# Attention followed by eight routed experts: the routing is issued by a running estimate of VectorE's time, and two experts' products are turned by TensorE

## The chip, the cores and the metric

The kernel is written in Bass for one core of a Trainium2 chip. The metric is device time in microseconds (us) of one execution. Kernel before: 892.86 us, the median of three runs (891.03, 892.86, 893.77). Each engine (TensorE, VectorE, ScalarE, GpSimd and SyncE; PE, DVE, ACT, POOL and SP in the profile) executes its own instructions strictly in the order in which the program lists them, and waits at an instruction until what that one needs is there. So the order of each list matters, and the change is one of order.

## The reference

Sigmoid attention of 8 batches and 12 heads makes 3584 rows of 768 numbers. The rows then go to eight experts. The routing is greedy over all (row, expert) pairs in falling order of their logit, and each expert takes exactly 448 rows:

```python
    order = np.argsort(-flat)
    for idx in order:
        tok, e = (int(idx) // E, int(idx) % E)
        if assigned[tok] >= 0 or counts[e] >= cap:
            continue
        assigned[tok] = e
        counts[e] += 1
    for e in range(E):
        mask = assigned == e
        h = np.maximum(x[mask] @ w1[e], 0.0)
        out[mask] = h @ w2[e]
```

`w1[e]` is 768x1024 and `w2[e]` 1024x768, in float32.

## The kernel before

**Attention** fills the first 280 us and is not touched. It ends with the rows in DRAM (`xs`) and the logits in SBUF.

**Routing** runs in eight phases, one an expert, and each phase finds the next expert that fills up, and its 448 rows. A phase (`Router.phase`) is nearly all VectorE work with a few short TensorE operations: take the former expert's rows out and make new keys (`remove`, `keys`, L306 to L158); turn the keys (TensorE, L167) and copy them (L170); search the threshold in 16 steps (L178 to L217), each step counting how many keys lie over three candidates; then `r_kap` (L222), a TensorE transpose of it (L229), the pick (L232 to L250), positions (TensorE L257, L262, L263; VectorE L259 to L268), a one-hot table (`r_oh`, L284) that TensorE turns into lists (32 small matmuls L289, then L296), and the list of row numbers `r_idx` (L298). Phase k+1 can be issued only after phase k.

**Experts.** With a list there, four gathers on GpSimd's queue bring an expert's rows (L625, tiles `xr`). Each block of 128 rows is turned in two halves: three TensorE transposes into a PSUM tile (L639, `tp`, two buffers), ScalarE copies the rounded part out (`xh`, L642), and VectorE makes the remainder (`xl`, L643), which frees the PSUM buffer. So there are eight such turns of three transposes an expert. The first product then takes 144 matmuls (L725, L727, L729) and the second 144 (L765, L767, L769). Weights stream in over SP's queue; ScalarE and GpSimd split them (`wh` L603, `wl` L605), GpSimd also makes `hl` (L737).

**Products.** For experts 0 to 6 VectorE turns each of the three product tiles in 32x32 blocks straight out of PSUM (`turn_y`, L666), four DMAs store it to DRAM (`ys`, L672), four more read rows back (L677), and GpSimd scatters them to the output (L681). Only the last expert is turned by TensorE: a ScalarE copy (L793), and per block of rows two transposes (L652) and a ScalarE copy (L657).

**What sets the order.** The loop over `moe(kx)` lists the matmuls; each `yield` tells the matmul's price (`MM` = 189 ns) and moves a model clock. Two other streams are woven in by that clock. The routing generator yields how long its last piece is thought to last, and the next piece is listed when the clock is past the last one by that and `SLACK`:

```python
                if t >= t_route:
                    t_route = t + next(route, 0) + SLACK
```

A search step has `T_DVE` = 2025 ns. Chores (gathers, turns, stores, scatters) have due times and one is listed at most every `CHORE_NS` = 1000 ns. At the end of an expert `flush` lists every chore that the next expert needs, at once. Inside `xturn` the VectorE instruction L643 is listed right behind the transposes and the ScalarE copy that it waits for.

Of the kernel before, what the change touches and what calls it, by code (L numbers as in the profile page):

```python
# [118 lines left out]
class Router:  # L119
# [42 lines left out]
    def search(self, pe):  # L162
# [10 lines left out]
        for st in range(16):  # L173
# [45 lines left out]
            if not pe:  # L219
                yield T_DVE  # L220
# [31 lines left out]
    def place(self):  # L252
# [7 lines left out]
        yield T_TOT  # L260
# [10 lines left out]
    def lists(self):  # L271
# [10 lines left out]
        nc.vector.tensor_tensor(K.mv[:, :, :8], os, K.tok[:, :, None].to_broadcast([112, 32, 8]), OP.mult)  # L282
        oh = wk.tile([112, 64, 32], F16, name="r_oh", bufs=1)
        nc.vector.tensor_tensor(oh, K.io64, rr[:, None, :].to_broadcast([112, 64, 32]), OP.is_equal)  # L284
        yield T_OH
# [7 lines left out]
        yield T_BT  # L293
# [30 lines left out]
    def phase(self, k):  # L324
        if k:
            self.remove()
        if k < 7:
            self.keys()
            yield T_KEYS
            yield from self.search(k == 0)  # L330
            yield T_KAP
            self.pick()
        else:
            self.left()
        yield T_PICK
        yield from self.place()
        yield from self.lists()


def moe_attention(tc, q, k, v, w_gate, w1, w2, out):  # L340
# [7 lines left out]
    with contextlib.ExitStack() as ctx:  # L348
# [202 lines left out]
        def routing():  # L551
            for kx in range(E):
# [6 lines left out]
                yield 0  # L559
# [68 lines left out]
        def xturn(kx, j, n, hf, wide):  # L628
# [12 lines left out]
            sl = (slice(None), slice(hf * 3, hf * 3 + 3), slice(j * 128, j * 128 + n))  # L641
            nc.scalar.activation(xh[sl], pv, AF.Copy)  # L642
            nc.vector.tensor_tensor(xl[sl], pv, xh[sl].bitcast(F32), OP.subtract)  # L643

        scat, chores = [], []
        MM = 189

        def untranspose(kx, yr, i, yt, j, n, t0=0, end=False):

            p = R.bank() if end and j % 2 else ps_t.tile([128, 512], F32, name="tp")  # L650
# [10 lines left out]
        def turn_y(kx, i, py):  # L661
# [4 lines left out]
            nc.vector.transpose(z.rearrange("p b (j d) -> p d b j", d=2),  # L666
                                py[:, :, :S].rearrange("p d (b t) -> p d b t", t=32))
# [5 lines left out]
            return store  # L673
# [31 lines left out]
        def moe(kx):  # L705
# [3 lines left out]
            for i in range(4):  # L709
                ph = ps_s.tile([128, 2, 512], F32, name="sc")  # L710
                cuts = ((0, 256), (256, S)) if kx + i == 0 else ((0, S),)
                mm = 107 if len(cuts) > 1 else MM
# [29 lines left out]
            if kx == E - 1:  # L742
# [3 lines left out]
            for i in range(3):  # L746
                last = (kx, i) == (E - 1, 2)
                for lo, hi in (((0, 256), (256, S)) if last else ((0, S),)):
                    py = ps_s.tile([128, 2, 512], F32, name="sc")
                    w = hi - lo  # L750
                    for j in range(2):
# [5 lines left out]
                        for d2 in range(2):  # L757
                            dsl = slice(d2 * 128, (d2 + 1) * 128) if kx == E - 1 else slice(d2, 256, 2)
# [22 lines left out]
                    if kx < E - 1:  # L781
                        extra[0] += Y_NS
                        chores.append((clock[0] + Y_WAIT, kx + 2, turn_y(kx, i, py)))
                        if i == 2:
                            for j, n in blocks():
                                chores.append((clock[0] + 2 * Y_WAIT + 1000, kx + 2,
                                               lambda j=j, n=n: y_row(kx, yr, j, n)))
                            for j, n in blocks():
                                chores.append((clock[0] + Y_LATE + 2600 * j, kx + 2,
                                               lambda j=j, n=n: scatter(kx, yr, j, n)))  # L790
                        break
# [7 lines left out]
        clock, extra = [0.0], [0.0]  # L799
# [8 lines left out]
        for j, n in blocks():  # L808
            for hf in range(2):
                if j < 2:  # L810
                    xturn(0, j, n, hf, True)
                else:
# [4 lines left out]
        t_route, t_chore = FIRST, 1500.0  # L817
        for kx in range(E):
# [40 lines left out]
            flush(kx + 1)  # L859
        flush(E + 1)  # L860
# [27 lines left out]
```

## Time and profile before

| What | Value |
|---|---|
| Median of three runs | 892.86 us |
| The profiled execution: its time, and its span | 898.64 us, 896.7 us |
| PE busy, share of the span | 841.6 us, 94% |
| DVE busy | 557.1 us, 62% |
| ACT busy | 412.3 us, 46% |
| POOL busy | 466.8 us, 52% |
| Mean granted TensorE clock | 0.969 |

The sums below are made against the profiled execution. It is 5.8 us longer than the median of the runs, so what the sums give is a difference, and it is taken off the median. The span runs from the first to the last instruction. A matmul's end is modelled and matmuls overlap, so "PE busy" says little; the time between the starts of matmuls is what is used. "Granted clock" is the share of full speed at which TensorE was allowed to run.

### The profile page before, as it was taken

To read this page: it belongs to the slowest core of one execution; us is meant where nothing else is said; L and a number is where in the kernel's file an instruction comes from. 1 tells how busy PE (TensorE), PEld (TensorE's weight loads), DVE (VectorE), ACT (ScalarE), POOL (GpSimd) and SP (SyncE) were. 2 spreads that over 40 slices of the span, in tenths; PEclk is the share of its full clock that TensorE was granted. 3 is DMA by queue.
4 is the path that set the end of the run, shared out by engine and by line. 5 is a ranking of instruction groups with operands and counts; after the bars stand their busy time and mean duration, and the time that the engine had idled before them with its cause. 6 is when DMAs were issued, how large, how long until landed. Compare 5 with 4: busy or idle time off the path is not lost.

```text
span 896.7 us, 16051 instructions
## 1 busy us (share of the span) xinstructions
PE 841.6 (94%) x5339; PEld 641.5 (72%) x5339; DVE 557.1 (62%) x2076; ACT 412.3 (46%) x532; POOL 466.8 (52%) x446
## 2 busy tenths in 40 slices
PE   6999999999998849989998998998999999999996
PEld 3455555455454539978987987997998888999996
DVE  4566555555555978868678858948957975233110
ACT  6777777777775723413413412332242342451432
POOL 9744444444400026834862873595485685653561
PEclk9999999999999969998997998999899999999998
DMA  9867666666603863374465455554546646835631
GB/s 173 166 141 152 143 124 126 133 124 126 132 18 113 276 196 99 95 201 151 141 202 160 120 183 142 157 185 139 179 147 200 182 147 200 242 127 174 214 109 62
DMA packets 246066, 136.83 MB, mean 153 GB/s; under 512 B 183360, under 2 KB 232512, under 8 KB 245984
## 3 DMA queue, kind: packets, MB, share of 16 engines
q1 hardware_dynamic: 233248, 102.31, 43.7%
q0 software_dynamic: 10880, 33.28, 12.1%
q8 instruction: 42, 0.69, 0.3%
q10 hardware_dynamic: 1856, 0.23, 0.2%
q14 instruction: 40, 0.33, 0.1%
HBM read 104.10 MB, written 31.65 MB: 151 GB/s over the span
## 4 chain that ended last, share of the span: by engine, by line
PE 75%; DVE 12%; issue 6%; POOL 4%; DMA 2%; ACT 1%; SPq 0%; POOLq 0%; DVEq 0%; ACTq 0%
PE tp L457 13%; PE sc L433 11%; PE sc L727 8%; PE sc L725 8%; PE sc L729 8%; PE sc L767 6%; PE sc L765 6%; PE sc L769 5%; DVE r_junk L178 4%; PE tp L463 2%; PE sc L443 2%; POOL wl L605 2%; DVE xl L643 1%; PE tp L639 1%; PE tp L478 1%
## 5 line engine op out<-in xcount | busy, mean ns | idle before, releaser
L605 POOL TENSOR_TENSOR wl<-wr,wh 128x768 fp32r<-128x768 f32 (+1 forms) x96 | 204.2, 2140 | 84.4 <-ACT wh L603 83.8
L423 ACT ACTIVATE at<-sc,bias 128x896 f32<-128x896 f32 x168 | 161.3, 1005 | 66.8 <-PE sc L443 38.4
L383 POOL DMA_DIRECT2D nkq<-in_q_dram x188 | 118.2, 645 | 116.2 <-DVE kqT L408 104.6
L727 PE MATMUL sc<-xl,wh 128*128 128x448 f32 (+2 forms) x396 | 148.4, 375 | 3.1 <-DVE xl L643 3.1
L725 PE MATMUL sc<-xh,wh 128*128 128x448 f32 (+2 forms) x396 | 148.8, 376 | 0.0
L729 PE MATMUL sc<-xh,wl 128*128 128x448 f32 (+2 forms) x396 | 148.3, 374 | 0.0
L769 PE MATMUL sc<-hh,wl 128*128 128x448 f32 (+2 forms) x400 | 147.4, 369 | 0.0
L603 ACT ACTIVATE wh<-wr 128x768 fp32r<-128x768 f32 (+1 forms) x112 | 101.0, 936 | 99.7 <-PE sc L767 69.6
L765 PE MATMUL sc<-hh,wh 128*128 128x448 f32 (+2 forms) x400 | 145.8, 364 | 0.5 <-ACT yt L694 0.5
L767 PE MATMUL sc<-hl,wh 128*128 128x448 f32 (+2 forms) x400 | 146.2, 366 | 0.0
L178 DVE TENSOR_SCALAR_CACHE_REDUCE r_junk<-r_KE,r_T 128x224 bf16<-128x224 f32 x315 | 123.4, 442 | 0.1
L737 POOL TENSOR_TENSOR hl<-yt,hh 128x896 fp32r<-128x896 f32 x32 | 68.2, 2130 | 100.8 <-ACT yt L736 100.8
L457 PE MATMUL tp<-at,nv 128*64 128x448 f32 x576 | 118.8, 548 | 0.0
L733 ACT ACTIVATE hh<-sc 128x896 fp32r<-128x896 f32 x32 | 29.4, 919 | 152.7 <-PE sc L729 152.7
L417 DVE TENSOR_TENSOR kqL<-kqT,kqH 128x896 fp32r<-128x896 f32 (+1 forms) x49 | 52.5, 1073 | 58.3 <-ACT kqH L416 58.2
L727 PEld LDWEIGHTS sc<-xl,wh 128*128 128x128 f32 x396 | 77.9, 197 | 11.0 <-DVE xl L643 4.0
L625 POOL DMA_INDIRECT xr<-xs,r_idx x32 | 32.1, 1002 | 100.4 <-ACT wh L603 80.2
L725 PEld LDWEIGHTS sc<-xh,wh 128*128 128x128 f32 x396 | 77.9, 197 | 7.2
L729 PEld LDWEIGHTS sc<-xh,wl 128*128 128x128 f32 x396 | 77.8, 197 | 7.1
L767 PEld LDWEIGHTS sc<-hl,wh 128*128 128x128 f32 x400 | 77.8, 194 | 5.4 <-issue 1.5
L765 PEld LDWEIGHTS sc<-hh,wh 128*128 128x128 f32 x400 | 77.7, 194 | 4.6 <-ACT yt L694 0.6
L769 PEld LDWEIGHTS sc<-hh,wl 128*128 128x128 f32 x400 | 77.8, 194 | 3.6
(166 smaller groups left out, 1166.8 us busy)
## 6 DMA issues: line engine op xcount, KB each, us to landing
wr<-in_moe_w_dram SPq DMA_DIRECT2D x64, 384.0 KB, 4.2
wr<-in_moe_w_dram SPq DMA_DIRECT2D x48, 512.0 KB, 4.0
nkq<-in_k_dram SPq DMA_DIRECT2D x192, 56.0 KB, 2.6
xs<-xr SPq DMA_DIRECT2D x32, 336.0 KB, 3.4
nkq<-in_q_dram POOLq DMA_DIRECT2D x188, 56.0 KB, 2.7
ys<-yt SPq DMA_DIRECT2D x84, 112.0 KB, 2.9
nv<-in_v_dram SPq DMA_DIRECT2D x92, 96.0 KB, 2.6
xr<-ys SPq DMA_DIRECT2D x21, 384.0 KB, 5.3
```

Source lines behind the costliest of these rows:

```text
L178: nc.vector.tensor_scalar(junk, KE, T[:, i:i + 1].bitcast(F32), None, OP.is_ge, OP.add, accum_out=cnt[:, i:i + 1])
L383: qn.dma_start(t[o:o + 32, n], rws[x])
L423: nc.scalar.activation(a, p[:, :, :S], AF.Sigmoid, bias=bias, scale=1 / math.sqrt(D))
L457: nc.tensor.matmul(p[j * 64:j * 64 + 64, :S], nat["v", b, g][:, h0 + j, c, :], AT[b, pr, c][:, j, :], start=(c == 0), stop=(c == 2 and pr ...
L603: nc.scalar.activation(hi, raw[u], AF.Copy)
L605: eng.tensor_tensor(lo, raw[u], hi.bitcast(F32), OP.subtract)
L725: nc.tensor.matmul(ph[:, f, lo:hi], wh[:, a, fs], xh[:, dd, lo:hi], start=st, stop=False)
L727: nc.tensor.matmul(ph[:, f, lo:hi], wh[:, a, fs], xl[:, dd, lo:hi], start=False, stop=False)
L729: nc.tensor.matmul(ph[:, f, lo:hi], wl[:, a, fs], xh[:, dd, lo:hi], start=False, stop=en)
L765: nc.tensor.matmul(py[:, d2, :w], wh[:, a, dsl], h1, start=st, stop=False)
L767: nc.tensor.matmul(py[:, d2, :w], wh[:, a, dsl], h2, start=False, stop=False)
L769: nc.tensor.matmul(py[:, d2, :w], wl[:, a, dsl], h1, start=False, stop=(j == 1 and a == 3))
```

## The change

1. Pacing of the routing. `T_...`, `SLACK`, `FIRST` are gone. Every piece of routing yields two numbers: what it costs VectorE, and how long VectorE then waits for TensorE. `dve[0]` is a running model of the time at which VectorE is done with all that was listed so far. `go_on` lists the next piece when the model clock is within `LEAD` (300 ns) of that time, or, where VectorE waits for TensorE, `GAP` (250 ns) past it. A search step is now two pieces, the counting at 1150 ns and the rest at 940 ns; before it was one piece.
2. The model clock: a matmul is priced at 203 ns for 189, and transposes advance the clock too.
3. VectorE's `xl` and its product transposes are listed later than the TensorE and ScalarE work that they wait for (`after`, lags of 900 and 500 ns), so that they stand between pieces of routing, and their cost goes into the model.
4. Experts 0 and 1 (`Y_FIRST` = 2) have their products turned by TensorE, as the last expert has; experts 2 to 6 as before.
5. The four gathers of the second expert (kx 1) are listed at once, not one every 1500 ns. The chore interval depends on what the last chore put on TensorE (300, 1100 or 1500 ns, for 1000).

```diff
-T_KEYS, T_KE, T_STEP, T_DVE, T_KAP, T_PICK, T_TOT, T_OH, T_BT = 3600, 2100, 2050, 2025, 500, 2600, 600, 3800, 600
-SLACK = 150
-CHORE_NS = 1000
+PE_NS, OH_NS, GAP, LEAD = 600, 1700, 250, 300
-FIRST = 4000.0
-Y_NS, Y_WAIT, Y_LATE = 1100, 5000, 29000
+Y_FIRST, Y_WAIT, Y_LATE, X_NS = 2, 5000, 29000, 1500
...
-                yield T_STEP
+                yield 0, 0
+            else:
+                yield 1150 + 430 * (st == 0), 0
+            if pe:
...
-            if not pe:
-                yield T_DVE
+            if not pe and st < 15:
+                yield 940 + 850 * (st == 0), 0
...
+        yield 2050, 0
         oh = wk.tile([112, 64, 32], F16, name="r_oh", bufs=1)
         nc.vector.tensor_tensor(oh, K.io64, rr[:, None, :].to_broadcast([112, 64, 32]), OP.is_equal)
-        yield T_OH
+        yield 2300, OH_NS
...
-            yield T_KEYS
+            yield 4600, PE_NS
             yield from self.search(k == 0)
-            yield T_KAP
+            yield 1100, PE_NS
             self.pick()
...
-        yield T_PICK
+        yield 2550, PE_NS
...
+            clock[0] += 3 * 110
             nc.scalar.activation(xh[sl], pv, AF.Copy)
-            nc.vector.tensor_tensor(xl[sl], pv, xh[sl].bitcast(F32), OP.subtract)
+
+            def low():
+                nc.vector.tensor_tensor(xl[sl], pv, xh[sl].bitcast(F32), OP.subtract)
+            after(900, 170 + n * 3, low)
...
-        MM = 189
+        MM = 203
...
+        def after(lag, cost, f):
+            later.append((clock[0] + lag - LEAD, cost, f))
+            hand_out()
+
+        def hand_out(end=False):
+            while later and (end or later[0][0] <= clock[0]):
+                _, cost, f = later.pop(0)
+                dve[0] = max(dve[0], clock[0] + LEAD) + cost
+                f()
+
+        def by_dve(kx):
+            return Y_FIRST <= kx < E - 1
...
-            if kx == E - 1:
+            if not by_dve(kx):
                 yr = [xp.tile([128, DM], F32, name="xr", bufs=XR_BUFS) for _ in blocks()]
...
-                            dsl = slice(d2 * 128, (d2 + 1) * 128) if kx == E - 1 else slice(d2, 256, 2)
+                            dsl = slice(d2 * 128, (d2 + 1) * 128) if not by_dve(kx) else slice(d2, 256, 2)
...
+        clock[0], dve[0], seg[:] = 0.0, 2400.0, [0, 2400.0]
+        t_chore = 1500.0
+
+        def go_on():
+
+            while clock[0] >= (seg[1] + GAP if seg[0] else dve[0] - LEAD):
+                cost, wait = next(route, (0, -1))
+                if wait < 0:
+                    seg[:] = 1, 1e9
+                    return
+                dve[0] = max(dve[0], clock[0] + seg[0]) + cost
+                seg[:] = wait, dve[0]
...
-                    chores.append((t0 + 1500 * j, kx + 1, lambda j=j, n=n: gather(kx + 1, j, n)))
+                    if kx:
+                        chores.append((t0 + 1500 * j, kx + 1, lambda j=j, n=n: gather(kx + 1, j, n)))
+                    else:
+                        gather(1, j, n)
...
-                t_route += extra[0]
-                extra[0] = 0.0
-                if t >= t_route:
-                    t_route = t + next(route, 0) + SLACK
+                hand_out()
+                go_on()
...
-                        t_chore = t + CHORE_NS
+                        t_chore = t + (300, 1100, X_NS)[min(2, int(clock[0] - t) // 110 - 1 if clock[0] > t else 0)]
```

What that does to the lists, at two places.

TensorE at the border between expert 0 and expert 1. `xr` are the gathered rows, `rt` routing, `yt` expert 0's products. Before, all eight turns of expert 1's rows (24 transposes) stand in one block behind the last matmul of expert 0:

```order
L769 MATMUL sc<-hh,wl 128x448
L639 MATMUL tp<-ident,xr 128x128 x18
L639 MATMUL tp<-ident,xr 128x64 x6
L725 MATMUL sc<-xh,wh 128x448
L727 MATMUL sc<-xl,wh 128x448
```

In the changed kernel the last rows there are these, and four more turns stand ahead of them, six matmuls apart:

```order
L640 MATMUL tp<-ident,xr 128x128 x3
L792 MATMUL sc<-hh,wh 128x448
L794 MATMUL sc<-hl,wh 128x448
L796 MATMUL sc<-hh,wl 128x448
...
L640 MATMUL tp<-ident,xr 128x128 x3
L640 MATMUL tp<-ident,xr 128x64 x6
L752 MATMUL sc<-xh,wh 128x448
L754 MATMUL sc<-xl,wh 128x448
L756 MATMUL sc<-xh,wl 128x448
L658 MATMUL tp<-ident,yt 128x128 x2
```

Five of the eight turns moved ahead of the border, three are left at it, and expert 0's product transposes (`yt`) are new on TensorE.

VectorE at the same border, in the search for expert 2. `r_junk` is the counting, `r_T` the next candidates. Before:

```order
L211 TENSOR_SCALAR r_T<-c_kk,r_J 128x3
L666 STREAM_TRANSPOSE yt<-sc 128x2x448
L643 TENSOR_TENSOR xl<-tp,xh 128x3x128 x6
L643 TENSOR_TENSOR xl<-tp,xh 128x3x64 x2
L178 TENSOR_SCALAR r_junk,c_CN<-r_KE,r_T 128x224 x3
```

And in the changed kernel:

```order
L175 TENSOR_SCALAR r_junk,c_CN<-r_KE,c_c_425 128x224 x3
L647 TENSOR_TENSOR xl<-tp,xh 128x3x128
L194 STREAM_TRANSPOSE r_ct<-c_CN 128x32
...
L211 TENSOR_SCALAR r_T<-c_kk,r_J 128x3
L647 TENSOR_TENSOR xl<-tp,xh 128x3x128 x2
L175 TENSOR_SCALAR r_junk,c_CN<-r_KE,r_T 128x224 x3
L647 TENSOR_TENSOR xl<-tp,xh 128x3x128
```

The eight `xl` are spread over three pieces of the search, and the product transpose is gone from VectorE's list for experts 0 and 1.

The places of the routing's TensorE operations, counted in expert matmuls from the first one, move like this (expert 0 ends at 324, and then an expert ends every 288: 612, 900, 1188, 1476, 1764, 2052):

| Phase, for expert | Keys turned (L167): before, now | `r_kap` turned (L229) | List ready (L296) | Turns at the border itself |
|---|---|---|---|---|
| 1 | before the first in both | 243, 210 | 293, 266 | 8 of 8, 3 of 8 |
| 2 | 314, 292 | 516, 470 | 572, 529 | 7, 0 |
| 3 | 593, 553 | 795, 730 | 845, 790 | 3, 0 |
| 4 | 872, 817 | 1074, 1014 | 1124, 1074 | 2, 0 |
| 5 | 1151, 1101 | 1353, 1298 | 1403, 1358 | 0, 0 |
| 6 | 1424, 1386 | 1632, 1583 | 1682, 1643 | 0, 0 |

More of the change, by code (lines that the diff above doesn't have):

```diff
@@ L259, in place @@
         nc.vector.tensor_copy(tot, p[:64, :1].to_broadcast([64, 112]))
-        yield T_TOT
+        yield 270, PE_NS
         p = self.bank()
@@ L292, in lists @@
         nc.vector.tensor_copy(bt, p[:, :64])
-        yield T_BT
+        yield 230, PE_NS
         p = self.bank()
@@ L558, in routing @@
                 R.ei = None
-                yield 0
+                yield 160, 0
         route = routing()
@@ L641, in xturn @@
             sl = (slice(None), slice(hf * 3, hf * 3 + 3), slice(j * 128, j * 128 + n))
+            clock[0] += 3 * 110
             nc.scalar.activation(xh[sl], pv, AF.Copy)
-            nc.vector.tensor_tensor(xl[sl], pv, xh[sl].bitcast(F32), OP.subtract)
+            def low():
+                nc.vector.tensor_tensor(xl[sl], pv, xh[sl].bitcast(F32), OP.subtract)
+            after(900, 170 + n * 3, low)
         scat, chores = [], []
-        MM = 189
+        MM = 203
         def untranspose(kx, yr, i, yt, j, n, t0=0, end=False):
+            clock[0] += 220
             p = R.bank() if end and j % 2 else ps_t.tile([128, 512], F32, name="tp")
@@ L659, in untranspose, with turn_y @@
                 scatter(kx, yr, j, n)
-        def turn_y(kx, i, py):
+        def after(lag, cost, f):
[8 more added lines that the diff above has]
+            return Y_FIRST <= kx < E - 1
+        def turn_y(kx, i, py, yr):
             z = hp.tile([128, 2, S], F32, name="yt", bufs=YT_BUFS).rearrange("p n t -> p (n t)")
             z = z.rearrange("p (b c) -> p b c", c=64)
-            nc.vector.transpose(z.rearrange("p b (j d) -> p d b j", d=2),
-                                py[:, :, :S].rearrange("p d (b t) -> p d b t", t=32))
             def store():
@@ L672, in store, with turn @@
                     nc.sync.dma_start(v[i, q], z[32 * q:32 * q + 32])
-            return store
+            def turn():
+                nc.vector.transpose(z.rearrange("p b (j d) -> p d b j", d=2),
+                                    py[:, :, :S].rearrange("p d (b t) -> p d b t", t=32))
+                chores.append((clock[0] + Y_WAIT, kx + 2, store))
+                for j, n in blocks() if i == 2 else ():
+                    chores.append((clock[0] + 2 * Y_WAIT + 1000, kx + 2, lambda j=j, n=n: y_row(kx, yr, j, n)))
+                for j, n in blocks() if i == 2 else ():
+                    chores.append((clock[0] + Y_LATE + 2600 * j, kx + 2, lambda j=j, n=n: scatter(kx, yr, j, n)))
+            after(500, 1150, turn)
         def y_row(kx, yr, j, n):
@@ L711, in moe @@
                 cuts = ((0, 256), (256, S)) if kx + i == 0 else ((0, S),)
-                mm = 107 if len(cuts) > 1 else MM
+                mm = 119 if len(cuts) > 1 else MM
                 for lo, hi in cuts:
@@ L780, in moe @@
                         break
[L781 to L790, printed above, removed]
+                    if by_dve(kx):
+                        turn_y(kx, i, py, yr)
                         break
@@ L797, in moe @@
                                            untranspose(kx, yr, i, yt, j, n, lo, last)))
-        clock, extra = [0.0], [0.0]
+        clock, dve, seg, later = [0.0], [0.0], [0, 0.0], []
         while 0 not in listed:
@@ L811, in moe_attention @@
                     xturn(0, j, n, hf, True)
+                    hand_out(True)
                 else:
@@ L816, in moe_attention @@
                     next(route)
-        t_route, t_chore = FIRST, 1500.0
+        clock[0], dve[0], seg[:] = 0.0, 2400.0, [0, 2400.0]
[8 more added lines that the diff above has]
+                seg[:] = wait, dve[0]
         for kx in range(E):
@@ L835, in flush @@
                     c[2]()
+                    hand_out(True)
+                hand_out(True)
             for step, cost in enumerate(moe(kx)):
@@ L859, in moe_attention @@
             flush(kx + 1)
+        hand_out(True)
         flush(E + 1)
```

## The prediction

> **What bounds the kernel now.** I read the page's slices first, then busy time by expert, the chain of waits and the list of waits, then the timeline at the places that these name.
>
> ```profile
> PE   6999999999998849989998998998999999999996
> PEclk9999999999999969998997998999899999999998
> ```
>
> TensorE is the bound throughout: its row stands at 8 and 9. In the expert part (from slice 15) the granted clock dips again and again. One stretch for each expert, first matmul to first matmul, with the instructions on the tile `sc`:
>
> ```profile
> 332.83:406.65 73.82, 64.17 (x330) 58.09 (x330) 4.81 (x6) 8.23 (x11) 0.96 0.49 143
> 406.65:480.08 73.43, 62.96 (x288) 56.01 (x288) 3.32 (x3) 6.91 (x8) 0.94 0.51 157
> 555.00:622.65 67.65, 65.03 (x288) 56.32 (x288) 2.23 (x2) 6.91 (x8) 0.96 0.59 175
> 763.72:825.55 61.83, 60.82 (x289) 54.37 (x288) 3.35 (x3) 6.91 (x8) 1.00 0.63 192
> sum 492.72, PE 448.56 PEld 392.24 DVE 23.70 ACT 49.70; mean PE 64.08 PEld 56.03 DVE 3.39 ACT 7.10
> ```
>
> Expert 6 (763.72) has the same 288 matmuls and 24 row transposes, no routing left, clock 1.00: 61.83 us. That is the floor of an expert. Experts 0 to 5 take 68 to 75. Where the difference goes shows in the chain at the border between experts 0 and 1:
>
> ```profile
> 400.29 1.11 DVE yt L666
> 401.40 0.46 DVE xl L643
> 401.90 0.56 PE tp L639 x3
> 402.48 0.50 ACT xh L642
> 403.00 0.57 DVE xl L643
> 403.62 1.38 PE tp L639 x6
> ```
>
> TensorE turns rows, ScalarE copies, VectorE subtracts, and only then is a PSUM buffer free for the next turn: a loop of 403.62 - 401.90 = 1.72 us in which TensorE works 0.38 (priced below). VectorE was late to begin with, since a product transpose stood ahead. The waits, and what they do to the clock:
>
> ```profile
> DVE r_km L232 <- PE rt L229: 34.9, 7, 8.6
> PEld tp L639 <- DVE xl L643: 18.8, 24, 2.5
> 459.87 1.13 PE L289 MATMUL rt<-r_oh,c_mv 112*32 112x64 f16 x32 [1.34 <-DVE r_oh L284]
> 532.24 1.11 PE L289 MATMUL rt<-r_oh,c_mv 112*32 112x64 f16 x32 [1.37 <-DVE r_oh L284]
> 403.70:410.60 6.90, 6.30 (x23) 5.02 (x24) 5.13 (x24) 3.11 (x6) 2.69 (x2) 0.52 0.31 86
> 461.10:464.50 3.40, 3.40 (x18) 2.94 (x19) 2.27 (x7) 0.85 (x1) 0.64 (x1) 1.00 0.18 47
> 475.40:485.70 10.30, 8.90 (x31) 7.26 (x31) 8.21 (x36) 4.08 (x8) 3.61 (x2) 0.52 0.47 121
> 533.40:536.90 3.50, 3.50 (x12) 2.67 (x12) 2.00 (x7) 0.00 (x0) 1.47 (x2) 0.55 0.19 65
> ```
>
> After the border waits the clock is at half for 6.9 us (403.70) and 10.3 us (475.40). One wait of 1.37 us was followed by 3.5 us at half clock (533.40), one of 1.34 was not (461.10). So a wait of this size may cost its own length and 1.7 us more. And VectorE waits 34.9 us in seven phases, 5 each, for TensorE to reach the turn of `r_kap`: the routing is listed later than VectorE could do it. That slack is what the change spends.
>
> **The change part by part.** Prices first:
>
> ```profile
> 771.10:778.54 7.44, 7.44 (x37) 6.76 (x37) 1.52 (x1) 3.19 (x4) 4.64 (x2) 1.00 1.01 318
> 778.54:787.50 8.96, 8.96 (x52) 8.13 (x52) 3.28 (x5) 5.16 (x8) 3.92 (x2) 1.00 0.85 241
> 796.24:825.55 29.31, 29.31 (x145) 27.95 (x145) 2.24 (x2) 1.73 (x2) 1.00 0.57 180
> 862.14:870.24 8.10, 8.10 (x44) 7.31 (x44) 0.00 (x0) 3.05 (x6) 6.49 (x10) 1.00 0.35 147
> ```
>
> Each of the first two and the last holds 36 matmuls. Twelve row transposes add 8.96 - 7.44 = 1.52, 0.127 each. 144 matmuls take 29.31, 0.2035 each; 36 are 7.33, so the 8 product transposes of the last row add 0.77, 0.19 a pair. Over an expert a matmul is (61.83 - 24 x 0.127) / 288 = 0.204. Routing puts the 32 small matmuls on TensorE (1.13 above) and four short ones, about 0.5: 1.6 a phase.
>
> *Products of experts 0 and 1 on TensorE.* 24 pairs, 4.6 us on the bounding engine. VectorE loses six transposes of 1.11. SP loses 32 transfers, ScalarE gains six tile copies and 24 row copies on an engine that is busy a third of the time in these stretches. Of the pairs 6 fall into expert 0, 13 into expert 1, 5 into expert 2.
>
> *Turns off the border.* Three of expert 1's eight turns and none of the later ones stay there. The other turns stand 6 matmuls apart, 1.22 + 0.38 = 1.6 us, about the loop's length, so they hide. I leave one unhidden loop at the first border: 1.72 - 0.38 = 1.3, and one stretch of half clock, 1.7.
>
> *The search is listed closer.* This is the part that costs. A search step is now priced 1150 + 940 = 2090 ns. What it takes:
>
> ```profile
> 611.77 0.36 PE L167 MATMUL rt<-ident,r_KT 112*128 112x112 f32 x2
> 616.43 0.44 DVE L178 TENSOR_SCALAR_CACHE_REDUCE r_junk<-r_KE,r_T 128x224 bf16<-128x224 f32 x1
> 618.75 1.01 DVE L643 TENSOR_TENSOR xl<-tp,xh 128x384 fp32r<-128x384 f32 x2
> 654.88 0.15 DVE L222 TENSOR_SCALAR r_kap<-r_J 128x1 int32<-128x1 int32 x1
> ```
>
> One step is 618.75 - 616.43 = 2.32 us, with no gap on VectorE. From the keys' turn to the end of `r_kap` are 655.03 - 611.77 = 43.26, one product transpose in it: 42.2 without (phases 2 and 3), 44.4 with two (phases 4 to 6). On TensorE's list now stand between the same two, in phase 3, 177 matmuls, 21 row transposes and 8 pairs: 36.1 + 2.7 + 1.5 = 40.3; in phases 4 and 5, 197 and 21: 42.9; in phase 6, 197 and 24: 43.2; in phase 2, 178, 24, 6 pairs and the border's wait: 41.8. So TensorE comes to `r_kap` early and waits: 0.4, 1.9, 1.5, 1.5, 1.2 us in phases 2 to 6. Before, VectorE waited. Phase 1 runs from the start:
>
> ```profile
> 332.83:344.48 11.65, 11.29 (x78) 10.46 (x79) 1.47 (x3) 1.31 (x3) 0.87 0.59 191
> 332.83:372.50 39.67, 39.31 (x216) 36.61 (x217) 1.47 (x3) 8.23 (x11) 0.96 0.45 136
> 338.75 0.56 DVE L643 TENSOR_TENSOR xl<-sc,xh 128x384 fp32r<-128x384 f32 x1 [0.83 <-ACT xh L642]
> 375.77 0.21 DVE L217 TENSOR_SCALAR r_J<-r_acc,r_J 128x1 int32<-128x1 int32 x1
> ```
>
> TensorE has done 210 matmuls (and six transposes on `sc`) at 372.5. VectorE ended its last step at 375.98; a product transpose that follows falls away, and of its early waits for `xh`, of which the row shows one of 0.83, some 1.3 us goes as counting now stands between them. So `r_kap` at 374.8 and a wait of 2.4 us, with one stretch of half clock, 1.7. What is late next: nothing, the list is ready 58 matmuls ahead of the border, not 31. For the half clock behind the 1.9 of phase 3 I add half a stretch, 0.85; the shorter ones stay near the 1.34 that had none.
>
> [...]
>
> *Gathers.* The first turn follows the list's matmul by 25 to 28 matmuls, 5.1 us and up.
>
> ```profile
> 391.58 0.20 PE L296 MATMUL rt<-c_SEL,r_bt 128*64 128x4 f16 x2
> 392.25 0.97 POOL L625 DMA_INDIRECT xr<-xs,r_idx  x1 [3.31 <-DVE rt L306]
> xr<-xs,r_idx POOLq DMA_INDIRECT x32, 4.7
> 740.83 0.20 PE L296 MATMUL rt<-c_SEL,r_bt 128*64 128x4 f16 x2
> 743.19 5.52 DMA xr<-xs,r_idx
> ```
>
> Issue 0.67 behind L296 and 4.7 to land: 5.4. Phase 7 had 2.36 + 5.52 = 7.9, behind a scatter. So 0 to 2.8 a phase; I take 0.3, near the first, and 0.3 for a late `r_oh`. Listing expert 1's gathers in a row puts blocks 1 to 3 earlier on GpSimd than their turns need, so it costs nothing; a `wl` behind them waits at most 4 issues.
>
> The sum, us:
> - Expert 0: 11.65 + 252 x 0.2035 + 1.6 + 3.05 + 6 x 0.19 + 2.4 + 1.7 + 1.3 + 1.7 = 75.8
> - Expert 1: 61.83 + 1.6 + 2.5 + 0.4 + 0.6 = 66.9
> - Expert 2: 61.83 + 1.6 + 1.0 + 1.9 + 0.85 + 0.6 = 67.8
> - Experts 3 and 4: 61.83 + 1.6 + 1.5 + 0.6 = 65.5 each
> - Expert 5, with two phases: 61.83 + 3.2 + 1.2 + 0.6 = 66.8
> - Expert 6: 61.83
>
> Together 470.1 for 492.72: 22.6 less. Expert 7 and the end stay. Taken off the median, 892.86 - 22.6 = 870.
>
> **The rivals.**
>
> *VectorE is in time after all.* Pieces listed among the waits, and `xl` between counting and the rest, could hide what the row-by-row sum doesn't. Then the picks' waits (8.9) and their half clock (2.55) go: 859. Against it: the steps run without gaps now, there is nothing to hide in.
>
> *The gathers take the border's place.* If the landing of phase 7 is the rule, TensorE waits 2.8 at the first turn of five experts and pays 1.7 of clock each time: 22.5 for my 1.5, so 891, no change to speak of. For it: turns come closer behind the list than before. Against: only one of seven first gathers was issued that late.
>
> *The pick's wait breaks the clock* (slower). TensorE's list is strict, so all matmuls behind L229 stand still in each of six phases. If each such wait is followed by 10.3 us at half clock, as at 475.40, that is 5.1 x 6 = 30.6 for my 2.55: 898. It turns slower where the half clock costs over (22.6 + 2.55) / 6 = 4.2 us a pick. For it: my waits of 1.2 to 2.4 lie around the 1.37 that tripped. Against: the long stretches followed several waits in a row.
>
> **How the numbers follow.** The forecast 0.70, VectorE in time 0.10, gathers 0.12, broken clock 0.08. A difference under 0.3% can't be told here. Forecast and first rival are faster, half of the gathers' case is within 0.3%: faster 0.86, same 0.06, slower 0.08. The range: down to 859, the first rival; up to 886, where the picks' half clock or the gathers cost 16 more than I take.
>
> **What would show it.** Right: the first matmul of expert 1 near 408 us, of expert 7 near 803; no TensorE waits on `xl` at borders 2 to 6; new waits of L229 on `r_kap`, 1 to 2.5 us in at least four phases, and hardly any of `r_km` on L229; clock dips at picks, not at borders. Wrong: `r_km` still waiting microseconds for L229 (a step is cheaper in its new place), or the first turn of each expert waiting for `xr`, or half clock longer than 3.5 us behind each pick.

## The result

| | Median, us | Lowest to highest | Runs |
|---|---|---|---|
| Kernel before | 892.19 | 891.03 to 893.77 | 4 |
| Changed kernel | 904.33 | 899.88 to 904.79 | 4 |

The changed kernel takes 1.0124 times as long, 95% interval 1.0087 to 1.0160. Forecast were 870 us, between 859 and 886: wrong in size and in sign. The profiled execution of the changed kernel took 904.54 us (span 902.8), right at its median.

Busy time and the slices of the changed kernel's page:

```profile
PE 840.3 (93%) x5387; PEld 640.0 (71%) x5387; DVE 545.1 (60%) x2070; ACT 425.6 (47%) x562; POOL 464.8 (51%) x446
PE   6999999999998749999979999989989999999996
PEclk9999999999999969999989999989999999999999
```

The dips of the border are gone from the expert part, but PE now has 7 and 8 where it had 9, and PEclk dips once in each of three experts. By expert, first matmul to first matmul (the instructions on tile `sc`, as in the prediction):

```profile
332.54:407.24 74.70, 68.23 (x330) 57.54 (x331) 1.43 (x3) 10.91 (x14) 0.96 0.40 124
407.24:486.06 78.82, 67.68 (x288) 54.49 (x289) 0.00 (x0) 8.73 (x10) 0.94 0.35 116
486.06:553.95 67.89, 63.28 (x290) 53.60 (x288) 2.21 (x2) 7.82 (x9) 1.00 0.46 142
553.95:626.41 72.46, 64.36 (x289) 55.51 (x288) 3.34 (x3) 6.91 (x8) 0.95 0.56 164
626.41:698.53 72.12, 63.88 (x289) 55.52 (x288) 3.34 (x3) 6.91 (x8) 0.95 0.55 165
698.53:768.88 70.35, 63.23 (x290) 53.81 (x288) 3.33 (x3) 6.92 (x8) 1.00 0.55 170
768.88:831.01 62.13, 60.80 (x290) 54.38 (x289) 3.35 (x3) 6.92 (x8) 1.00 0.62 190
```

| Expert | 0 | 1 | 2 | 3 | 4 | 5 | 6 | Sum |
|---|---|---|---|---|---|---|---|---|
| Forecast | 75.8 | 66.9 | 67.8 | 65.5 | 65.5 | 66.8 | 61.8 | 470.1 |
| Measured | 74.7 | 78.8 | 67.9 | 72.5 | 72.1 | 70.4 | 62.1 | 498.5 |

Experts 0, 2 and 6 came out within 1.1 us. Experts 1, 3, 4 and 5 are 11.9, 7.0, 6.6 and 3.6 us too long. The list of waits says on what (engine, tile and line, what it waited for: total us, times, the longest):

```profile
PE tp L640 <- DMA xr<-xs,r_idx: 21.0, 7, 6.0
PE rt L229 <- DVE r_kap L222: 10.7, 7, 2.1
DVE r_km L232 <- PE rt L229: 2.9, 7, 0.4
DVE r_KE L167 <- PE rt L164: 17.2, 6, 8.6
PE tp L640 <- DVE xl L647: 0.8, 1, 0.8
```

The picks' waits (`r_kap`) are there as forecast, the border waits on `xl` are gone (12.2 us before on the same turns), and `r_km` fell from 34.9 to 2.9. New is the first row: TensorE at a turn waits for the gathered rows `xr`. About 5 us of it lie ahead of expert 0, in every version alike. The rest are 6.05, 3.52, 3.80 and 1.88 us in experts 1, 3, 4 and 5, just the four that are too long; in expert 5 it is the third turn that waits, in the others the first. The next turn of keys (L164) stands behind that turn in TensorE's list and started after it (in expert 1 at 469.49, behind 468.44), so VectorE stood still for up to 8.6 us too (`r_KE`).

Why the rows were late in expert 1 shows in the timeline there, here cut to the lines that matter (start, duration, engine and line; in brackets how long the engine was idle before and what ended it):

```profile
454.67 2.39 POOL L606 TENSOR_TENSOR wl<-wr,wh 128x1024 fp32r<-128x1024 f32 x1 [7.82 <-ACT wh L604]
456.95 0.16 DVE L299 TENSOR_SCALAR r_idx<-rt 128x4 int32<-128x4 f32 x1 [2.34 <-PE rt L297]
...
459.80 0.37 ACT L663 COPY xr<-tp 64x256 f32<-64x256 f32 x1 [0.87 <-PE tp L658]
460.07 1.06 ACT L604 ACTIVATE wh<-wr 128x1024 fp32r<-128x1024 f32 x1
461.20 2.36 POOL L606 TENSOR_TENSOR wl<-wr,wh 128x1024 fp32r<-128x1024 f32 x1 [4.14 <-ACT wh L604]
463.72 0.99 POOL L626 DMA_INDIRECT xr<-xs,r_idx  x1 [0.16 <-issue]
468.44 0.87 PE L640 MATMUL tp<-ident,xr 128*128 128x128 f32 x3 [6.05 <-DMA xr<-xs,r_idx]
470.10 0.39 DVE L167 COPY r_KE<-rt 128x224 f32<-128x224 f32 x1 [8.59 <-PE rt L164]
```

The list `r_idx` is ready at 457.11. The gather stands on GpSimd behind a `wl`; that `wl` waits 4.14 us for its `wh`; and `wh` stands in ScalarE's list behind the row copies L663 of expert 0's product, each of which waits for TensorE (0.87 us before the one at 459.80). So the gather is issued at 463.72, 6.6 us after the list, and the turn starts 4.72 us after that, when the rows have landed. The turn had its place only 23 matmuls behind the list.

In experts 3, 4 and 5 it is another thing that stands ahead. Expert 3, the same view:

```profile
593.42 0.16 DVE L299 TENSOR_SCALAR r_idx<-rt 128x4 int32<-128x4 f32 x1 [2.35 <-PE rt L297]
593.44 2.40 POOL L606 TENSOR_TENSOR wl<-wr,wh 128x1024 fp32r<-128x1024 f32 x1
596.03 0.99 POOL L708 DMA_INDIRECT out_dram<-xr,r_idx  x1 [0.16 <-issue]
597.33 0.98 POOL L626 DMA_INDIRECT xr<-xs,r_idx  x1 [0.31 <-DVE rt L152]
598.61 0.91 POOL L708 DMA_INDIRECT out_dram<-xr,r_idx  x1 [0.22 <-issue]
602.20 0.90 PE L640 MATMUL tp<-ident,xr 128*128 128x128 f32 x3 [3.52 <-DMA xr<-xs,r_idx]
```

A `wl` and the scatters of the former expert's product (L708) stand before and between the gathers. The scatters keep their due time, 29 us behind the product, while the list now comes some 50 matmuls earlier. Before the change they were over by then: the last of the four is the row below, and the list was ready at 606.43.

```profile
602.78 1.69 POOL L681 DMA_INDIRECT out_dram<-xr,r_idx  x1 [0.17 <-issue]
```

What the waits cost on top, by windows of the granted clock (third number from the right):

```profile
376.00:379.40 3.40, 3.40 (x11) 3.02 (x10) 1.64 (x7) 0.00 (x0) 0.00 (x0) 0.51 0.00 0
440.90:444.30 3.40, 3.40 (x11) 3.01 (x11) 2.40 (x10) 0.98 (x2) 3.40 (x2) 0.50 0.48 150
464.80:471.60 6.80, 3.16 (x11) 2.88 (x12) 1.46 (x6) 0.49 (x1) 2.81 (x3) 0.50 0.77 259
601.30:608.10 6.80, 5.90 (x20) 5.22 (x21) 3.12 (x12) 0.98 (x2) 4.06 (x3) 0.50 1.05 289
673.00:679.80 6.80, 5.10 (x17) 4.56 (x18) 1.28 (x4) 0.98 (x2) 4.29 (x4) 0.50 1.01 331
```

The first two follow the picks of phases 1 and 2, the other three a late turn. What of the last three lies behind the wait runs at half speed: 471.6 - 468.44 = 3.2, 608.1 - 602.2 = 5.9 and 679.8 - 674.7 = 5.1 us, 14.2 together. In such a stretch matmuls start 0.373 us apart (PE timeline at 376.63, 377.00, 377.37), at full clock 0.205. So 45% of it is lost: 6.4 us, and 1.5 for each stretch of 3.4.

### The profile page after: what moved, and what is told of

It reads as the page before. It is cut to its first block, busy times and chain, and to the rows that moved or that the text cites. A ratio compares the mean times of both kernels' runs of the same rounds, so it can differ in the third digit from the quotient of the medians.

```text
span 902.8 us, 16113 instructions
## 1 busy us (share of the span) xinstructions
PE 840.3 (93%) x5387; PEld 640.0 (71%) x5387; DVE 545.1 (60%) x2070; ACT 425.6 (47%) x562; POOL 464.8 (51%) x446
## 3 DMA queue, kind: packets, MB, share of 16 engines
q0 software_dynamic: 10880, 33.28, 11.9%
## 4 chain that ended last, share of the span: by engine, by line
PE 58%; DVE 20%; issue 9%; POOL 7%; DMA 4%; ACT 1%; SPq 0%; POOLq 0%; DVEq 0%; ACTq 0%
PE tp L458 13%; PE sc L434 11%; DVE r_junk L175 9%; PE sc L792 6%; PE sc L796 6%; PE sc L794 6%; POOL wl L606 5%; DMA xr<-xs,r_idx 3%; PE tp L464 2%; PE tp L640 2%; PE sc L444 2%; PE sc L754 2%; PE sc L756 2%; PE sc L752 2%; DVE r_j L202 1%
## 5 line engine op out<-in xcount | busy, mean ns | idle before, releaser
L424 ACT ACTIVATE at<-sc,bias 128x896 f32<-128x896 f32 x168 | 161.4, 1005 | 66.9 <-PE sc L444 38.5
L792 PE MATMUL sc<-hh,wh 128*128 128x448 f32 (+2 forms) x400 | 150.8, 377 | 0.5 <-ACT yt L721 0.5
L794 PE MATMUL sc<-hl,wh 128*128 128x448 f32 (+2 forms) x400 | 148.7, 372 | 0.0
L754 PE MATMUL sc<-xl,wh 128*128 128x448 f32 (+2 forms) x396 | 145.2, 367 | 0.5 <-DVE xl L647 0.5
L752 PE MATMUL sc<-xh,wh 128*128 128x448 f32 (+2 forms) x396 | 144.4, 365 | 0.0
L756 PE MATMUL sc<-xh,wl 128*128 128x448 f32 (+2 forms) x396 | 144.0, 364 | 0.0
L754 PEld LDWEIGHTS sc<-xl,wh 128*128 128x128 f32 x396 | 75.0, 189 | 7.0 <-DVE xl L647 1.1
L752 PEld LDWEIGHTS sc<-xh,wh 128*128 128x128 f32 x396 | 75.1, 190 | 6.1 <-ACT xh L644 0.2
L756 PEld LDWEIGHTS sc<-xh,wl 128*128 128x128 f32 x396 | 75.0, 189 | 5.6
L458 PEld LDWEIGHTS tp<-at,nv 128*64 128x64 f32 x576 | 37.0, 136 | 59.2 <-issue 56.7
```

Of the source, the lines that this page charges most:

```text
L424: nc.scalar.activation(a, p[:, :, :S], AF.Sigmoid, bias=bias, scale=1 / math.sqrt(D))
L458: nc.tensor.matmul(p[j * 64:j * 64 + 64, :S], nat["v", b, g][:, h0 + j, c, :], AT[b, pr, c][:, j, :], start=(c == 0), stop=(c == 2 and pr ...
L752: nc.tensor.matmul(ph[:, f, lo:hi], wh[:, a, fs], xh[:, dd, lo:hi], start=st, stop=False)
L754: nc.tensor.matmul(ph[:, f, lo:hi], wh[:, a, fs], xl[:, dd, lo:hi], start=False, stop=False)
L756: nc.tensor.matmul(ph[:, f, lo:hi], wl[:, a, fs], xh[:, dd, lo:hi], start=False, stop=en)
L792: nc.tensor.matmul(py[:, d2, :w], wh[:, a, dsl], h1, start=st, stop=False)
```

## The experiments

The theory was that the loss is the first turns that wait for `xr`, because the gathers stand behind other work in the lists of GpSimd and ScalarE (A in the expectations). The rivals: the picks' waits on `r_kap` with what they do to the clock; and the products on TensorE. Each expectation names those that it is about. Each experiment is the changed kernel with the edit shown, unless the text says otherwise. Times are medians; ratios are to the kernel before, timed on the same chip (893.13 us for 1, 3, 4 and 6; 892.24 for 5, 7, 8 and 9; 892.78 for 2 and 10).

**1. Turns later behind the list.** `lag` is the time by which the model sets the first turn behind the list. Nothing is done to the gathers.

```diff
-                lag = max(5000, min(14000, start + 40000 - t0))
+                lag = max(10000 if kx else 5000, min(14000, start + 40000 - t0))
```

> The changed kernel with one number altered: row turns of experts 2 to 6 stand at least 10000 ns of the model clock behind the list, not 5000 (24 to 28 matmuls more, still ahead of the border but for two of them). Theory A (the loss is TensorE standing at the first turn until the gather has landed): the four waits on xr (6.05, 3.52, 3.80, 1.88, together 15.3 us) fall below 2 in total, the half-clock stretches at 465, 601 and 673 go (about 7 us more), time 882 within 4. Theory B (VectorE's routing chain sets the pace and the gathers only fill a wait that is there anyway): waits on r_kap grow from 10 to about 25 us and the time stays at 900 to 905.

Measured: 880.40 us, 0.9864 (0.9820 to 0.9907). That is in A's range. One number turns 12 us more into 13 us less. Waits, and the timeline at the place of the 6.05 us:

```profile
PE rt L229 <- DVE r_kap L222: 10.3, 7, 2.1
PE tp L640 <- DMA xr<-xs,r_idx: 5.5, 3, 5.0
```

```profile
453.26 0.16 DVE L299 TENSOR_SCALAR r_idx<-rt 128x4 int32<-128x4 f32 x1 [2.34 <-PE rt L297]
460.06 1.00 POOL L626 DMA_INDIRECT xr<-xs,r_idx  x1 [0.16 <-issue]
464.51 0.52 PE L640 MATMUL tp<-ident,xr 128*128 128x128 f32 x3 [0.29 <-DMA xr<-xs,r_idx]
```

The gather is as late as before, 6.6 us behind the list, but the turn comes later and waits 0.29. The picks' waits are untouched (10.3 for 10.7), so they are not the loss. In the profiled execution the clock is full from the first matmul of expert 0 through all seven experts, behind the picks too, some 3 us at which the edit did not aim. That is luck of this one execution (last section): its mean clock is 0.991, that of the other three 0.987 and 0.988.

**2. The same, half the dose.** `lag` at least 7500.

```diff
-                lag = max(5000, min(14000, start + 40000 - t0))
+                lag = max(7500 if kx else 5000, min(14000, start + 40000 - t0))
```

> Half the dose of the lag: least lag 7500 ns where the changed kernel has 5000 and the first experiment 10000. First turns then stand 34 to 37 matmuls behind the list for 23 to 28, 2.3 us more. Theory A (a turn waits exactly as long as its gather is late behind it): the waits on xr of 6.05, 3.52, 3.80 and 1.88 us fall to 3.7, 1.2, 1.5 and 0, and one or two of the three half-clock stretches that follow them go with them: 904 - 9 - 5 = 890, between 886 and 894. Theory B (it is no sum of waits: once a turn waits at all the clock and the order behind it are lost): as the changed kernel, over 898. Waits on r_kap as before in both, 1.3 to 2.1.

Measured: 887.78 us, 0.9954 (0.9940 to 0.9968), in the range of theory A. The waits are 3.79, 0.68, 1.40 and 1.08 us, 6.95 in all for 6.4 expected. The last was not expected: it is now the first turn that waits there, not the third.

**3. The search listed further apart**, as near as the price of a step allows to what it takes (2330 ns for 2090). The picks should stop waiting.

```diff
-                yield 1150 + 430 * (st == 0), 0
+                yield 1220 + 430 * (st == 0), 0
...
-                yield 940 + 850 * (st == 0), 0
+                yield 1110 + 680 * (st == 0), 0
```

> The changed kernel with a search step priced at what it takes, 1220 + 1110 = 2330 ns for 2090. Theory A: waits on r_kap fall from 10.0 us to below 2, the half clock at 376 and 441 goes, lists come 17 to 93 matmuls later, and from expert 3 on five to seven turns stand at the border again (1.3 us a turn and half clock): time 893 to 903. Theory C (the underpriced step is the cause of the whole loss): time below 885.

Measured: 888.97 us, 0.9959 (0.9938 to 0.9980), lower than A's range by 4 us and not as low as C, the underpriced step as the whole loss (below 885). Something was overlooked that the next rows show:

```profile
PE tp L640 <- DVE xl L647: 9.9, 14, 1.1
PE tp L640 <- DMA xr<-xs,r_idx: 7.7, 4, 4.9
PE rt L229 <- DVE r_kap L222: 0.7, 1, 0.7
```

The picks' waits are gone. So are most of the waits on `xr`: the later lists come when the scatters are through, and the first gather of experts 2 to 6 is issued 0.27 us behind the list. In their place the turns run into the border again and wait 9.9 us on `xl`. So this edit moves all three, and tells less than it was to tell.

**4. All products by VectorE.** The new pacing and the row of gathers stay, the products of experts 0 and 1 go back.

```diff
-Y_FIRST, Y_WAIT, Y_LATE, X_NS = 2, 5000, 29000, 1500
+Y_FIRST, Y_WAIT, Y_LATE, X_NS = 0, 5000, 29000, 1500
```

> The changed kernel with the products of experts 0 and 1 turned by VectorE as before (Y_FIRST 0). Theory A': ScalarE's product copies hold back wh, so GpSimd's wl and the gathers behind it; without them the 6 us wait on xr in expert 1 falls below 1, while waits on r_kap in phases 2 and 3 grow by 2 each; waits on xr in experts 3 to 5 stay: time 896 to 902. Theory D (24 more pairs of transposes on TensorE are the loss): only 4.6 us of TensorE work goes and the wait on xr in expert 1 stays: 899.

Measured: 880.94 us, 0.9849 (0.9800 to 0.9898): 15 us better than expected. That the wait in expert 1 goes was expected and came, but those of experts 3 and 4 nearly went too (1.38 and 1.06). With product transposes on VectorE all lists come later, by 26 matmuls in phase 2 and 43 in phase 4, and the first gather of every expert is issued 0.27 us behind its list. In expert 3:

```profile
589.32 0.16 DVE L299 TENSOR_SCALAR r_idx<-rt 128x4 int32<-128x4 f32 x1 [2.34 <-PE rt L297]
589.75 0.99 POOL L626 DMA_INDIRECT xr<-xs,r_idx  x1 [2.62 <-DVE rt L307]
595.95 0.55 PE L640 MATMUL tp<-ident,xr 128*128 128x128 f32 x3 [1.38 <-DMA xr<-xs,r_idx]
```

What is left of the wait is the landing, 595.95 - 589.75 = 6.2 us for a median of 4.5.

**5. The other half alone.** The kernel before, with its old pacing, and only the products of experts 0 and 1 turned by TensorE (against the kernel before):

```diff
-            if kx == E - 1:
+            if kx < 2 or kx == E - 1:
...
-                    if kx < E - 1:
+                    if 2 <= kx < E - 1:
```

> The kernel before with one part of the change alone: the products of experts 0 and 1 turned by TensorE, in place of VectorE and the way through DRAM; the old pacing stays. Lists come 12 to 42 matmuls earlier than before, so the border turns of experts 2 to 4 go. TensorE has 4.6 us more work. Theory A: scatters and wl stand among the gathers here too, the first turn stands 28 to 33 matmuls behind the list, so waits on xr of 1 to 3 us come up in experts 1 to 5; waits of TensorE on r_kap stay below 2 in total, for the steps are listed 12 matmuls apart (2.4 us for 2.32). Time 882 to 893. If moving products to TensorE is itself the loss: 897 or more.

Measured: 879.78 us, 0.9877 (0.9846 to 0.9908). That is 2 us below A's range, with 6.4 us of waits on `xr` in three experts. So products on TensorE are no loss; alone they gain 12 us. Its waits:

```profile
PE tp L639 <- DVE xl L643: 3.0, 5, 0.8
PE tp L639 <- DMA xr<-xs,r_idx: 11.6, 5, 4.9
```

The first row is the finding: the waits at the border, 12.2 us before, go to 3.0 by this part alone, and to 1.5 by the pacing alone (experiment 4). Both parts take away the same waits, so their gains don't add up. What does add up is how early the lists come: phase 4 has its list at matmul 1124 before, 1117 in experiment 4, 1082 here, 1074 in the changed kernel.

**6. Scatters earlier**, due 20 us behind the product instead of 29.

```diff
-Y_FIRST, Y_WAIT, Y_LATE, X_NS = 2, 5000, 29000, 1500
+Y_FIRST, Y_WAIT, Y_LATE, X_NS = 2, 5000, 20000, 1500
```

> The changed kernel with the scatters due 20000 ns behind the product, not 29000, so that all four stand ahead of the next expert's gathers on GpSimd and not among them. Theory A'' (scatters in GpSimd's list are what delays the gathers of phases 4 to 6): waits on xr in experts 3, 4 and 5 (9.2 us together) fall below 3 and two half-clock stretches go, the 6 us wait in expert 1 stays: time 890 within 4. Rival (the landing itself is late, or wl stands ahead): waits stay over 7 us, time 902.

Measured: 895.78 us, 1.0030 (1.0008 to 1.0052), 6 us above the expected middle and outside its range (886 to 894). The waits of experts 3 to 5 fall from 9.2 to 1.87 + 2.60 + 0.45 + 0.84 = 5.8 us: the scatters were part of it. What stands ahead of the first gather now is `wl` alone, two of 4.74 us together in experts 3 and 4, and it is still issued 2.5 to 3.5 us behind its list.

**7. All experts' gathers listed at once.**

```diff
-                    if kx:
-                        chores.append((t0 + 1500 * j, kx + 1, lambda j=j, n=n: gather(kx + 1, j, n)))
-                    else:
-                        gather(1, j, n)
+                    gather(kx + 1, j, n)
```

> The changed kernel with the gathers of every expert listed at once behind the list, as it does for the second expert alone. The turns stand where they stood. Theory A with the scatters as the cause in phases 4 to 6: the gathers now stand ahead of the last scatters and of one or two wl, so the waits on xr in experts 3 to 5 (3.52, 3.80, 1.88) fall below 3 in total; in expert 1 one wl fewer stands ahead and the 6.05 falls to 2 to 4. Time 882 to 892. If the landing of the gathers, not their place in GpSimd's list, is what is late, the waits stay and so does the time, 902 to 905.

Measured: 890.00 us, 0.9981 (0.9966 to 0.9995). In expert 1 the gather comes ahead of the `wl` that waited for ScalarE:

```profile
455.37 0.16 DVE L299 TENSOR_SCALAR r_idx<-rt 128x4 int32<-128x4 f32 x1 [2.34 <-PE rt L297]
455.81 1.00 POOL L626 DMA_INDIRECT xr<-xs,r_idx  x1 [0.33 <-PE tp L658]
461.36 0.52 PE L640 MATMUL tp<-ident,xr 128*128 128x128 f32 x3 [0.73 <-DMA xr<-xs,r_idx]
```

0.73 us for 6.05, and expert 1 takes 72.0 us for 78.8. This shows the mechanism of expert 1 at its own place: the transfer is no faster (461.36 - 455.81 = 5.55 us from its issue to the turn, for 4.72), it is issued 0.27 us behind the list. Experts 3 and 4 still wait 3.51 and 1.93, with scatters and a `wl` ahead. Below 3 us in all was expected there, so the time is in the range, but only expert 1 did better than forecast.

**8. The second expert's gathers spaced again**, which undoes that part of the change alone.

```diff
-                    if kx:
-                        chores.append((t0 + 1500 * j, kx + 1, lambda j=j, n=n: gather(kx + 1, j, n)))
-                    else:
-                        gather(1, j, n)
+                    chores.append((t0 + 1500 * j, kx + 1, lambda j=j, n=n: gather(kx + 1, j, n)))
```

> The changed kernel with the second expert's gathers as chores every 1500 ns again (this part of the change undone alone). The gathers of that expert landed 1 us or more ahead of their turns in the changed kernel, so by every theory little moves: 902 to 907, with at most 2 us more waiting on xr in expert 0.

Measured: 902.15 us, 1.0115 (1.0099 to 1.0132), the same four waits (5.95, 3.62, 3.90, 2.14). That part neither helps nor harms.

The seven versions side by side. How late the first gather is issued behind its list (end of L299, or L298, to the start of L626, or L625), for the rows of each expert, and what the turns of these rows, which stand in the expert before, then wait on `xr` (waits over 0.4 us, in order of time):

| Version | Issued late, experts 1 to 6, us | TensorE waits on `xr`, us | Time |
|---|---|---|---|
| Before | 0.27, 0.27, 0.27, 0.61, 0.27, 1.97 | none | 892.2 |
| Changed | 0.27, 6.61, 0.78, 3.74, 4.54, 2.37 | 6.05, 3.52, 3.80, 1.88 | 904.3 |
| 1, lag 10000 | 0.27, 6.64, 0.77, 3.37, 3.92, 4.54 | none | 880.4 |
| 2, lag 7500 | 0.27, 6.64, 0.80, 3.40, 3.94, 4.56 | 3.79, 0.68, 1.40, 1.08 | 887.8 |
| 4, VectorE | 0.27 six times | 1.38, 1.06 | 880.9 |
| 5, old pacing | 1.17, 1.20, 0.27, 3.45, 4.21, 2.26 | 2.92, 1.97, 1.49 | 879.8 |
| 7, at once | 0.27, 0.27, 0.80, 3.95, 3.47, 2.24 | 0.73, 3.51, 1.93 | 890.0 |

For the rows of experts 1 to 5 the changed kernel, 1 and 2 have nearly the same lateness, and all in all they wait 15.25, nothing and 6.95 us: it is the distance of the turn from the list that turns lateness into time. (The 1.88 us of the changed kernel are the second gather's, issued at 744.18 behind a `wl` and a scatter.)

**9. Everything at once**: the steps of experiment 3, gathers at once, `lag` at least 7000, and closer pricing of the waits inside a phase.

```diff
-PE_NS, OH_NS, GAP, LEAD = 600, 1700, 250, 300
+PE_NS, OH_NS, GAP, LEAD = 450, 1300, 200, 300
...
-                yield 940 + 850 * (st == 0), 0
+                yield 1110 + 680 * (st == 0), 0
...
-                lag = max(5000, min(14000, start + 40000 - t0))
+                lag = max(7000 if kx else 5000, min(14000, start + 40000 - t0))
...
+                    gather(kx + 1, j, n)
```

(The step's first half, the gathers' other lines and `X_NS` = 1100 as well.)

> What the runs so far point to, together: a step priced at 2330 ns, gathers in a row for all experts, turns 7000 ns behind the list and 4 matmuls apart (1100 ns) for 6, and waits of VectorE on TensorE priced shorter (450, 1300, 200 for 600, 1700, 250). Waits on r_kap below 3 us in total, on xr below 3, no turn left at borders 2 to 4: time 868 to 877. If VectorE's chain sets the pace whatever the list says, it stays at 880.

Measured: 878.94 us, 0.9858 (0.9836 to 0.9879), 2 us over the range, and nearer to the rival's 880 (VectorE's chain sets the pace) than to it, so this run does not decide between them. The waits on `r_kap` are gone, and those on `xr` but for 1.76 us in expert 0. New ones stand where the list is made: TensorE waits for the one-hot table `r_oh` 2.49 and 1.85 us, and for `xl` at the borders behind experts 0, 4 and 5.

**10. In the middle**: a step of 2180 ns, gathers at once, `lag` at least 9000, `X_NS` = 1100.

```diff
-                yield 1150 + 430 * (st == 0), 0
+                yield 1180 + 430 * (st == 0), 0
...
-                yield 940 + 850 * (st == 0), 0
+                yield 1000 + 790 * (st == 0), 0
...
-                lag = max(5000, min(14000, start + 40000 - t0))
+                lag = max(9000 if kx else 5000, min(14000, start + 40000 - t0))
...
+                    gather(kx + 1, j, n)
```

> A step of 2180 ns, between the 2090 of the changed kernel and the 2330 with which r_kap had no waits; least lag 9000 ns, all gathers in a row, 1100 ns between chores. Theory A (waits on r_kap are a sum: 16 steps of 90 ns take 1.4 us from each of 1.97, 2.12, 1.40, 1.48, 1.32 and 1.37): no waits on xr, waits on r_kap of 0.5 to 0.7 us in two phases, no turns at the borders, 880.4 - 8.4 = 872, between 869 and 877. Theory B (what is taken from these waits comes back at r_oh, at the borders or in the clock, as with 2330): 878 to 882.

Measured: 875.08 us, 0.9803 (0.9787 to 0.9820), the shortest of all, 17 us below the kernel before and 29 below the changed one.

```profile
PE tp L640 <- DMA xr<-xs,r_idx: 5.4, 2, 5.2
PE rt L229 <- DVE r_kap L222: 4.8, 7, 1.7
PE tp L640 <- DVE xl L647: 2.4, 4, 0.8
```

It lies in A's range. Against experiment 1 the picks' waits fell by 5.5 us for 8.4 expected (1.03, 1.66, 0.43, 0.30 and 0.47 are left), and waits on `xl` rose by 1.0: 5.3 us of the 8.4 were gained. Its seven experts sum to 470.5 us.

## Why the prediction was wrong

**What bounds the kernel**: right. TensorE is busy for 94% of the span before and 93% in the changed kernel, and the large gains and losses are waits of TensorE and the clock behind them.

**Turns off the border**: right. First matmul of expert 1 at 407.24 (forecast 408), one wait of 0.84 on `xl` at the first border and none later. The half clock given to that border (1.7) didn't come.

**The picks' waits**: right in all, by phase but for one. Forecast 2.4, 0.4, 1.9, 1.5, 1.5 and 1.2, together 8.9; measured 1.94, 2.10, 1.85, 1.55, 1.27 and 1.32, together 10.0. Phase 2 was put 1.7 too low. Two were followed by 3.4 us at half clock, 1.5 lost each; 1.7 and 0.85 were forecast. So the slower rival, a broken clock behind every pick, is wrong.

**Products on TensorE**: right in that they cost little on TensorE: the kernel with them alone is 12 us shorter. What was missed is that they and the pacing remove the same waits (experiment 5), and that ScalarE's new copies, called harmless as it is "busy a third of the time", stand in its list ahead of a `wh`: in expert 1 that is what held up the gather.

**Gathers**: here the prediction failed. Its step "0 to 2.8 a phase; I take 0.3" stood against 6.05, 3.52, 3.80 and 1.88 us measured, and 6.4 us of half clock behind them: 15.25 + 6.4 = 21.7 us for 1.5. The rival "the gathers take the border's place" named the right wait, but took 2.8 us as the most and 0.12 as its chance. Two parts of the step were wrong:

- "Only one of seven first gathers was issued that late" is a row of the kernel before. How late a gather was issued here was set by what stood ahead of it on GpSimd, and by what those waited for on ScalarE: 0.27 us in expert 0, where GpSimd had been idle for 1.06 us, and 6.61 us in expert 1, behind two `wl`. The change moves the lists against just those: by 43 matmuls in phase 2 and by 50 in phase 4. The question was not how late gathers had been but who stands ahead of them in the new lists. That the scatters are due at a fixed 29 us behind the product could be read in the code, and that a `wl` may wait 7.82 us for ScalarE is a matter of the same list.
- "Listing expert 1's gathers in a row ... costs nothing; a `wl` behind them waits" looked at the side behind the gathers. The `wl` ahead of them was the one that counted, and the row made no difference (experiment 8).

**The sum.** The sum of the experts came out 28.4 us too low. Of that 13.75 are waits on `xr` (15.25 - 1.5) and 6.4 the half clock behind them. The other terms nearly cancel: picks 1.1 too low, their clock 0.5 too low, the first border 2.2 too high. Some 8.8 us stay (1.5 more by what was forecast for `r_oh`, on which no phase waited over 0.4 us), and no single wait over 0.4 us holds them. Most of them show in the starts of the matmuls. Next to the places where TensorE leaves its matmuls for a turn, a product or a piece of routing, two matmuls start 0.28 to 0.32 us apart for 0.205. Experts 1 to 5 of the changed kernel have 120 such steps, their waits taken off, and lose 12.2 us in them; expert 6, from which the floor was taken, has 11 and loses 1.05. That is 7.0 us more than the floor holds. So the floor of an expert with routing was too low; what the rest is stays open.

The seven experts of experiment 1 take 473.6 us for the 470.1 forecast, but that is in part luck, too. Its floor is too low in the same way, by some 10 us, and 7.4 us of forecast terms did not come: the picks' half clock (2.55), most of the first border (2.15), the gathers (1.2) and `r_oh` (1.5).

**The base.** 5.8 us are of another kind. The profiled execution of before was 5.8 us longer than the median. The difference was worked out against it, and taken off the median. Its mean granted clock is 0.969, and of 45 other executions of this kernel the longest (897.68 us) has 0.969 and the shortest (888.14 us) 0.982. That points to half clock as part of what made it longer, and this part was then counted as gain. 28.4 + 5.8 is 34.2 of the 34.3 us between 870 and 904.33.

## What to carry to other kernels

When a change makes one stream of work earlier, look up for each transfer that it triggers what stands ahead of it in the issuing engine's new list, and for each of those what it waits for in turn: their due times stay where they were. A consumer with a fixed place in a strict list should stand behind its producer by issue, landing and the lateness found there, here 10 us and not 5, which was worth 24 us. Two changes that each remove the same wait don't add their gains, but their side effects do add.

## What was not expected of the hardware

The same wait may or may not cost clock. At the first pick TensorE waits 1.94 us in the changed kernel and 1.97 in experiment 1, at the same place of the program. The changed kernel's clock is then at 0.51 for 3.4 us (the row 376.00 above). In experiment 1, the wait, and windows with TensorE's busy time and the clock:

```profile
374.16 0.32 PE L229 MATMUL rt<-ident,r_kap 128*112 128x128 f32 x1 [1.97 <-DVE r_kap L222]
```

```profile
370.00:373.41 3.41, 2.19 (x11) 1.00 0.26 93
373.41:376.83 3.42, 2.67 (x14) 1.00 0.00 0
434.86:438.27 3.41, 1.60 (x8) 1.00 0.48 148
438.27:441.69 3.42, 3.11 (x16) 1.00 0.56 161
```

Full speed, also behind the second pick's 2.12 us. The windows are cut where the clock of that trace changes, or multiples of 3.413 us from there. In each trace here all stretches at half clock in the expert part last 3.413 us or a multiple of it (but for one that the end of the program cuts short), and their starts lie whole multiples of 3.413 us apart: in the changed kernel 376.04, 440.90, 464.79, 601.32 and 673.01. That is a grid, and it lies differently in each trace: a stretch starts at 404.03 in the kernel before, 8.2 times 3.413 us from 376.04. In the changed kernel the 1.94 us fall into one window of it whole:

```profile
372.63:376.04 3.41, 1.47 (x9) 1.00 0.00 0
```

TensorE is idle for 57% of that window, and the next one runs at half clock. In experiment 1 the border of two windows, 373.41, cuts the 1.97 us in two (36% and 22% idle), and of the 2.12 us 1.81 fall into one window (53%). In the twelve traces 1670 windows between 345 and 832 us start at full clock. All 22 in which TensorE is idle for more than 56%, with matmul ends as the profile models them, are followed by half clock, and none of those under 30%. Of the 50 between, 7 are; the five lowest of these, at 37 to 48%, hold turns or the 32 small matmuls of a list.

So for the waits of 1.3 to 2.1 us in these traces the length alone did not tell: half clock followed 1.94 us in the changed kernel and 1.37 before (the row 533.40 of the prediction), none followed 1.97 and 2.12 in experiment 1 and 1.34 before. How much of a wait falls into one window told more, by the counts above, but not all: the 1.37 us stand in a window that is idle for 40% (530.32 to 533.73, TensorE busy 2.04 us), against 53% without half clock in experiment 1. As the grid lies differently in each trace, a forecast can, as I judge it from these counts, give such a wait only a chance.
